# Token scores of six batches: the transposed tokens made by VectorE and a trip through DRAM, eight products of 64 rows in place of 64 products of 32 rows, and a new order of the loop

## The chip, the core and the metric

The kernel runs on one core of a Trainium2 chip. A core has TensorE (PE in the profile: matrix products, with PEld for its weight loads), VectorE (DVE), ScalarE (ACT), GpSimd (POOL) and SyncE (SP, which here only issues transfers). They run at the same time and wait for each other by semaphores. Matrix products write into PSUM, which is cut into banks; everything else lives in SBUF or in DRAM. The metric is the time of one execution in microseconds (us) on the device. Lower is better.

## What is computed

Two stages follow each other. The first is a cross attention between 512 tokens `x` and 32 states in each of 8 batches and 8 heads of 64 features, in both directions:

```python
scores = scale * np.matmul(x, state.transpose(0, 1, 3, 2))     # 512 x 32 per batch and head
a = softmax(scores)                                            # over the 32 states
xread = np.matmul(a, state)
scores2 = scale * np.matmul(state, x.transpose(0, 1, 3, 2))    # the same numbers, transposed
a2 = softmax(scores2)                                          # over the 512 tokens
sread = np.matmul(a2, x)
```

The 512 rows of `xread` and the 32 rows of `sread` of a batch are put one after the other, with the 8 heads side by side as 512 features. The second stage is a gated feed-forward network over these 4352 rows (8 batches of 544): each row is divided by its root mean square and scaled by `rms_g`, multiplied by `w_gate` and by `w_val` (512 by 1536 each), the gate goes through `g * sigmoid(g)`, the two are multiplied, and the product goes through `w_out` (1536 by 512). All of it is float32.

## The kernel before

**Loop.** Batch 0 and the preparation of the weights run first, in an order of their own (`ORDER`). Then a loop over `b` from 1 to 7 does the feed-forward network of batch `b`'s tokens and, beside it, the attention of batch `b + 1`. I call one pass a turn. The 256 state rows of all batches come last (`STATES`).

**Order.** The work of a turn is written as generators, each a stream named by a letter, and the string `PERIOD` says letter by letter whose next step is issued. TensorE, VectorE and ScalarE keep the order that this string gives. GpSimd and the transfer queues of SP get theirs from the planner of the language, by dependencies. The streams are:

- `h`: TensorE's products of the hidden layer (`hidden_seven`, L734). There are six pairs of weight blocks per batch, and each pair has seven products in place of eight, in banks called x, y and z. The steps of a pair are x, z, then s1 (into x), s2 (into z), y, s3 (into x) and the last (into x).
- `t`: ScalarE's copies of the x, z and again x banks (L780, L783, L785) and the gate function (L787). `u`: VectorE's sums for the same pair (L796, L799, L811, L815, L821).
- `p`: the projection by `w_out` (`project_seven`, L896), also with seven products, each in two halves of 12 passes. `c`: ScalarE's copies of finished halves (L933), `k`: VectorE's sums of them (L941, L948), followed by the stores.
- `v` and `w`: TensorE's products that fold the states into the gate and value weights (`own_weights`, L588), which needs weights loaded by SP (`fetch`, L176). `x`: ScalarE's copies of them (L599) and GpSimd's sums (L614 to L617).
- `a`: the token side of the attention of the next batch (`tokens_read`): scores, softmax over states, read of the states (L458), square, mean and root (`rms_on_blocks`, L395 to L406, then L278 on GpSimd and L285), and the scaling of the weights (L471).
- `s`: the state side (`states_read`): softmax over tokens, a transpose by way of DRAM (L512, L515, L519), the read of the tokens (L530), and its transpose (L542).

**Scores of batches 2 to 7.** `scores_of_blocks` works on 32 by 32 blocks. [...] the states are loaded four times, once for each group of 32 partitions (`load_fours`, L114), and transposed as `stB` (L337); the tokens are transposed as `xB` by two instructions (L343). The contraction over 64 features is then split in two halves of 32 rows: 64 products of 32 rows by 32 columns over 128 tokens (L354), into four banks, two of the pool `aps` ("at") and two of the pool `vps` ("pv"). VectorE transposes each bank back into `eS` (L365) and ScalarE copies each into `sS` (L368). For L458 and the scaled weights the states are transposed once more by TensorE (L435). Tokens are loaded so that a partition group holds the tokens that this order needs (L122).

**Scores of batches 0 and 1.** `scores` has the whole transpose: one transpose of the states by TensorE (L296), 16 of the tokens by TensorE with copies by ScalarE (L306, L308), and eight products of 64 rows by 512 tokens (L315) into two banks.

**Buffers.** `aps`, `vps` and `fx` hold two banks each, `fy` and `fz` one. `xT`, which holds `xB` and later the squares, is a single buffer in SBUF. Loaded weights have three.

Of the kernel before, what the change touches and what calls it, by code (L numbers as in the profile page):

```python
# [8 lines left out]
F32 = mybir.dt.float32  # L9
# [8 lines left out]
P = 128  # L18
# [13 lines left out]
    "hhvttvhtxhuhuhxuxthuhtthuhhuthxhuxhuuhtthahuuthtuhuvhxutauhhtxutxhhuuhxhthvuuthh"  # L32
    "axttxuhuuhthuhxhuuuutahhuahutthtuuhuahuuhupaatuauhauupucaaaasaaaaaaapsacksppsasc"
    "aappacaacakpkakaupsaasaacaaspsakksaaaspkkpasawwsspxwxxckpxsxksxc"
# [9 lines left out]
def kernel(  # L44
# [55 lines left out]
    fours = {}  # L100
# [8 lines left out]

    def load_fours(b):  # L110

        fours[b] = one.tile([P, H, D], F32, name="fours")
        for g in range(4):
            nc.sync.dma_start(out=fours[b][Ns * g:Ns * g + Ns],  # L114
                              in_=state[b].rearrange("h n d -> n h d"))
# [37 lines left out]
    w_d = [scratch.tile([P, NI, 2, 2, P], F32, name="w_d%d" % mp) for mp in range(NM // 2)]  # L153
    e_d = [scratch.tile([4, Ns, 4, 8 * Ns], F32, name="e_d%d" % k) for k in range(2)]
# [136 lines left out]
    def scores(b, packed, soft):  # L291

        xb = x_sb[b]
        stT = one.tile([P, 4, Ns], F32, name="stT")
        tp = aps.tile([P, 4, Ns], F32, name="at")
        TE.transpose(out=tp.rearrange("p j n -> p (j n)"),  # L296
                     in_=packed.rearrange("p e d -> p (e d)"), identity=ident)
        yield
        VE.tensor_copy(stT, tp)
        yield "step"  # L300

        xT = one.tile([P, 4, NC, P], F32, name="xT", tag="xT")
        for c in range(NC):
            tp = aps.tile([P, 4, P], F32, name="at")
            for j in range(4):
                TE.transpose(out=tp[:, j, :], in_=xb[:, c, P * j:P * j + P], identity=ident)  # L306
            yield
            SE.copy(xT[:, :, c, :], tp)  # L308
            yield "step"


        sp = [aps.tile([P, S], F32, name="at") for e in range(2)]
        for j in range(4):
            for e in range(2):
                TE.matmul(out=sp[e][Ns * j:Ns * j + Ns, :], lhsT=stT[D * e:D * e + D, j, :],  # L315
                          rhs=xT[D * e:D * e + D, j].rearrange("p c t -> p (c t)"),
                          start=True, stop=True)
        yield


        sS = read[b] = two.tile([P, 2, NC, P], F32, name="sS")
        eS = soft["e"] = one.tile([P, 2, S // Ns, Ns], F32, name="eS", tag="eS")
        for e in range(2):
            VE.transpose(out=eS[:, e].rearrange("p k n -> p (k n)"), in_=sp[e])
            yield
            SE.copy(sS[:, e].rearrange("p c t -> p (c t)"), sp[e])
            yield "step" if e else None

        soft["st"] = stT
        soft["half"] = lambda e: eS[:, e]  # L330
        soft["back"] = lambda e: [(aT_s[b][:, e], eS[:, e].rearrange("p k n -> p (k n)"))]

    def scores_of_blocks(b, packed, soft):

        xb = x_sb[b]
        stB = one.tile([P, H, 2, Ns], F32, name="stB")
        VE.transpose(out=stB.rearrange("p h k n -> p (h k n)"),  # L337
                     in_=fours.pop(b).rearrange("p h d -> p (h d)"))
        yield

        xB = one.tile([P, NC, H, 2, Ns], F32, name="xB", tag="xT")
        for i in range(0, NC, 2):
            VE.transpose(out=xB[:, i:i + 2].rearrange("p c h k t -> p (c h k t)"),  # L343
                         in_=xb[:, i:i + 2].rearrange("p c f -> p (c f)"))
            yield


        sp = [(aps, vps)[g // 2].tile([P, 2, NC, Ns], F32, name=("at", "pv")[g // 2])
              for g in range(4)]
        for e in range(2):  # L350
            for k in range(2):
                for j in range(4):
                    for g in range(4):
                        TE.matmul(out=sp[g][Ns * j:Ns * j + Ns, e].rearrange("n c t -> n (c t)"),  # L354
                                  lhsT=stB[Ns * g:Ns * g + Ns, 2 * j + e, k, :],
                                  rhs=xB[Ns * g:Ns * g + Ns, :, 2 * j + e, k, :],
                                  start=(k == 0), stop=(k == 1), skip_group_check=True)
        yield

        sS = read[b] = two.tile([P, 2, NC, P], F32, name="sS")
        eS = one.tile([P, 4, 2, NC, Ns], F32, name="eS", tag="eS")
        for g in (2, 3, 0, 1):
            VE.transpose(out=eS[:, g].rearrange("p e c n -> p (e c n)"),  # L365
                         in_=sp[g].rearrange("p e c t -> p (e c t)"))
            yield
            SE.copy(sS[:, :, :, Ns * g:Ns * g + Ns], sp[g])  # L368
            yield "step" if g == 1 else None
        soft["half"] = lambda q: eS[:, 2 * q:2 * q + 2].rearrange("p g e c n -> p (g e c) n")  # L370
        soft["back"] = lambda q: [(aT_s[b][:, :, P * g:P * g + P],
                                   eS[:, g].rearrange("p e c n -> p e (c n)"))
                                  for g in (2 * q, 2 * q + 1)]
# [41 lines left out]
    def tokens_read(b):  # L415
        packed, soft = rows.pop(b), {}
        yield from (scores if b < 2 else scores_of_blocks)(b, packed, soft)
        half = soft["half"]
# [6 lines left out]
        for e in range(2):  # L425
            VE.reduce_max(out=m1[:, e], in_=half(e), axis=AXX)
            yield
            VE.tensor_tensor(out=half(e), in0=half(e), in1=along(m1, e), op=ALU.subtract)
            yield
            SE.activation(out=half(e), in_=half(e), func=ACTF.Exp, scale=SCALE)  # L430
            yield "step"
        stT_g[b] = two.tile([P, 4, Ns], F32, name="stT_g")
        if b > 1:
            soft["st"] = aps.tile([P, 4, Ns], F32, name="at")
            TE.transpose(out=soft["st"].rearrange("p j n -> p (j n)"),  # L435
                         in_=packed.rearrange("p e d -> p (e d)"), identity=ident)
            yield
        VE.tensor_tensor(out=stT_g[b], in0=soft["st"], in1=rms_g.unsqueeze(2).to_broadcast([P, 4, Ns]),
# [3 lines left out]
        for e in range(2):  # L442
            VE.reduce_sum(out=z1[:, e], in_=half(e), axis=AXX)
# [4 lines left out]
            VE.tensor_tensor(out=half(e), in0=half(e), in1=along(z1, e), op=ALU.mult)  # L448
            yield
            for to, blocks in soft["back"](e):  # L450
                VE.transpose(out=to, in_=blocks)
# [23 lines left out]
    def states_read(b):  # L475
# [13 lines left out]
        for e in range(2):  # L489
            to = e2[:, :, e].rearrange("p g c t -> p c g t")  # L490
            if b < 2:
                to = exps[:, e]
            SE.activation(out=to, in_=sS[:, e].rearrange("p c (g t) -> p c g t", t=Ns)
                          if b > 1 else sS[:, e], func=ACTF.Exp, scale=SCALE,
# [544 lines left out]
    for b in range(1, B):  # L1039
# [3 lines left out]
        if b + 1 < B:  # L1043
            load_fours(b + 1)
# [58 lines left out]
```

## Time and profile before

| | |
|---|---|
| time, median of 3 | 791.25 us (790.87 to 791.53) |
| profiled execution | 791.0 us, span 789.2 us, granted clock 0.998 |
| batch 0 and preparation, 0 to 141.5 us | TensorE busy 133.3 us |
| one turn, b = 1 to 6 | 85.38 us each, TensorE busy 84.92, VectorE 58.65, ScalarE 31.37, GpSimd 23.6 |
| last turn and state rows, from 653.8 us | 77.6 and 57.8 us |
| VectorE transposes | 128x256: 0.42 to 0.45 us; 128x512: 0.70; 128x1024: 1.24 |
| transfers, issue to landing | 1 MB of weights 5.2 us; 0.5 MB written by `e_d<-eB` 2.9; 128 KB read by `e2T<-e_d` 3.0 |

A page of the profile gives the busy time of each engine, the chain of work that ended last (followed back from the end, at each step to what released it), and groups of equal instructions by line. A row of the chain reads: start in us, length in us, engine, tile, line, number of instructions. In the rows of windows the first column is the stretch, then its length and each engine's busy time with its number of instructions. A product in float32 is two instructions ("passes") in the trace, so 64 products are 128 rows of matmul. "PE f L896" is TensorE writing a tile named `f` at line 896. "ACTq" and "SPq" are the sequencers of ScalarE and SyncE issuing a transfer.

The six turns from b = 1 to 6 have the same length to 0.01 us.

### The profile page before, as it was taken

The numbers are of one execution on the slowest core, as the hardware profiler recorded it, in microseconds if no ns is written. First come the engines' busy times: TensorE is split into PE (matmuls) and PEld (weight loads), VectorE is DVE, ScalarE is ACT, GpSimd is POOL, SyncE is SP. The second block draws the span as 40 slices with busy tenths as digits, with TensorE's granted clock in tenths as the row PEclk, the third lists the DMA queues.
The fourth block names the chain that finished last, engine by engine and source line by source line (L and its number), as shares of the span: only waits on it lengthen the run. The fifth ranks groups of instructions, "written<-read, shape, count | busy, mean of one in ns | idle before, by whom it ended". The sixth has DMA issues, their size and how long they took to land.

```text
span 789.2 us, 13508 instructions
## 1 busy us (share of the span) xinstructions
PE 774.4 (98%) x5394; PEld 593.0 (75%) x5394; DVE 545.2 (69%) x858; ACT 327.6 (42%) x548; POOL 173.8 (22%) x232
## 2 busy tenths in 40 slices
PE   6999999999999999999999999999999999999998
PEld 5643444788777877888778877787788877888996
DVE  4999997689538871888368953887288835781461
ACT  5998864543145322543154314432254315410320
POOL 2100003530164004410443016400441044300000
PEclk9999999999999999999999999999999999999999
DMA  9878864730274025521453038402521143201311
GB/s 287 235 272 302 276 191 167 218 122 1 87 243 168 2 70 180 182 69 43 151 184 121 0 92 255 152 1 68 206 100 55 41 157 126 105 7 41 114 54 27
DMA packets 73599, 102.07 MB, mean 129 GB/s; under 512 B 46913, under 2 KB 57665, under 8 KB 66625
## 3 DMA queue, kind: packets, MB, share of 16 engines
q1 hardware_dynamic: 67040, 94.33, 36.5%
q10 hardware_dynamic: 6496, 6.88, 2.8%
q8 instruction: 43, 0.70, 0.4%
q14 instruction: 20, 0.16, 0.1%
HBM read 82.84 MB, written 18.35 MB: 128 GB/s over the span
## 4 chain that ended last, share of the span: by engine, by line
PE 94%; DVE 2%; ACT 2%; issue 0%; DMA 0%; SPq 0%
PE f L734 38%; PE f L896 35%; PE f L836 5%; PE pv L630 4%; PE at L588 3%; PE pv L588 3%; PE at L530 1%; PE at L458 1%; PE at L354 1%; PE f L987 1%; PE pv L354 1%; PE at L285 0%; DMA rows<-in_state_dram 0%; PE at L306 0%; ACT ex L225 0%
## 5 line engine op out<-in xcount | busy, mean ns | idle before, releaser
L896 PE MATMUL f<-wo,hb 128*128 128x256 f32 x540 | 123.5, 381 | 3.0 <-ACT ot L933 3.0
L734 PE MATMUL f<-aT_s,v 128*128 128x256 f32 x504 | 122.5, 384 | 0.0
L896 PEld LDWEIGHTS f<-wo,hb 128*128 128x128 f32 x540 | 102.1, 190 | 18.9 <-ACT ot L933 5.6
L734 PEld LDWEIGHTS f<-aT_s,v 128*128 128x128 f32 x504 | 93.7, 190 | 24.9 <-issue 12.2
L796 DVE TENSOR_TENSOR g<-g,f 128x512 f32<-128x512 f32 (+1 forms) x96 | 61.9, 652 | 65.2 <-PE f L734 61.8
L734 PE MATMUL f<-aT_t,vs 128*128 128x256 f32 x336 | 87.1, 382 | 0.0
L933 ACT COPY ot<-f 128x256 f32<-128x256 f32 x60 | 21.3, 368 | 157.5 <-PE f L896 157.5
L896 PE MATMUL f<-wt,hs 128*128 128x256 f32 x360 | 82.2, 382 | 0.0
L278 POOL TENSOR_TENSOR ri<-ss,mhalf 128x4 f32<-128x4 f32 x8 | 9.3, 1157 | 330.5 <-DVE ss L406 223.8
L896 PEld LDWEIGHTS f<-wt,hs 128*128 128x128 f32 x360 | 67.3, 190 | 13.9 <-ACT ot L933 4.9
L787 ACT ACTIVATE hb<-g 128x1024 f32<-128x1024 f32 (+1 forms) x48 | 48.2, 1004 | 67.6 <-DVE g L796 67.6
L734 PEld LDWEIGHTS f<-aT_t,vs 128*128 128x128 f32 x336 | 63.3, 190 | 14.8 <-issue 5.9
L614 POOL TENSOR_TENSOR vs<-v 128x256 f32<-128x256 f32 x42 | 30.4, 725 | 137.3 <-ACT v L599 137.2
L799 DVE SCALAR_TENSOR_TENSOR hb<-hb,g 128x1024 f32<-128x1024 f32 x42 | 52.3, 1245 | 5.9 <-ACT hb L787 5.9
L785 ACT COPY g<-f 128x512 f32<-128x512 f32 (+1 forms) x48 | 26.9, 560 | 55.3 <-PE f L734 55.3
L599 ACT COPY v<-pv 128x512 f32<-128x512 f32 x42 | 23.7, 598 | 60.0 <-PE pv L588 60.0
L836 PE MATMUL f<-wo,hb 128*128 128x512 f32 x96 | 44.7, 600 | 0.0
L617 POOL TENSOR_TENSOR vs<-v,vs 128x256 f32<-128x256 f32 x42 | 44.7, 1063 | 0.0
L630 PE MATMUL pv<-aT_s,v 128*128 128x512 f32 x96 | 43.6, 594 | 0.0
L734 PE MATMUL f<-aT_t,v 128*128 128x256 f32 x168 | 43.1, 379 | 0.0
L734 PE MATMUL f<-aT_s,vs 128*128 128x256 f32 x168 | 43.1, 379 | 0.0
L896 PE MATMUL f<-wt,hb 128*128 128x256 f32 x180 | 42.6, 387 | 0.0
(152 smaller groups left out, 1290.9 us busy)
## 6 DMA issues: line engine op xcount, KB each, us to landing
w_m<-w_d SPq DMA_DIRECT2D x48, 1024.0 KB, 5.2
out_dram<-ot SPq DMA_DIRECT2D x56, 128.0 KB, 1.8
raw<-in_moe_w_val_dram SPq DMA_DIRECT2D x6, 1024.0 KB, 5.4
raw<-in_moe_w_out_dram SPq DMA_DIRECT2D x6, 1024.0 KB, 8.0
x_b<-in_x_dram SPq DMA_DIRECT2D x96, 64.0 KB, 2.5
w_d<-w_m SPq DMA_DIRECT2D x6, 1024.0 KB, 4.9
raw<-in_moe_w_gate_dram SPq DMA_DIRECT2D x5, 1024.0 KB, 7.1
e_d<-eB ACTq DMA_DIRECT2D x6, 512.0 KB, 2.9
```

What stands on the lines that cost most here:

```text
L588: TE.matmul(out=pv[e][Ns * j:Ns * j + Ns, :], lhsT=stT_g[b][D * e:D * e + D, j, :], rhs=w[D * e:D * e + D, j].rearrange("p m k f -> p (m k ...
L599: SE.copy(v[:, e].rearrange("p m k f -> p (m k f)"), pv[e])
L614: GE.tensor_tensor(out=vs[:, 0], in0=a21, in1=a22, op=ALU.add)
L617: GE.tensor_tensor(out=vs[:, 2], in0=a12, in1=vs[:, 1], op=ALU.subtract)
L630: TE.matmul(out=to[0], lhsT=lhs(i, k), rhs=r, start=(i == 0), stop=(i == len(rhs) - 1))
L734: TE.matmul(out=ps[:, i, 0:half], lhsT=l[:, i, :], rhs=r, start=(start and i == 0 and k == 0), stop=(k == len(lhs) - 1), skip_group_check= ...
L785: SE.copy(gates(q)[1], q["x"][:, :, 0:half])
L787: SE.activation(out=hb[:, 2 * mp:2 * mp + 2, 0:n].rearrange("p m (c t) -> p m c t", c=2), in_=q["g"][:, :, :, 0:half], func=ACTF.Silu if s ...
L796: VE.tensor_tensor(out=to, in0=to, in1=q[ps][:, :, 0:half], op=ALU.add)
L799: VE.scalar_tensor_tensor(out=h, in0=h, scalar=1.0, op0=ALU.add, op1=ALU.mult, in1=q["g"].rearrange("p m c t -> p m (c t)"))
L836: TE.matmul(out=banks[r], lhsT=hb[:, m, P * r:P * r + P], rhs=wo[:, m, :], start=(m == 0), stop=(m == NM - 1))
L896: TE.matmul(out=banks[name][:, r, :], lhsT=lhs(k)[:, P * r:P * r + P], rhs=rhs(k), start=(start and r == 0 and k == 0), stop=(k == HM - 1) ...
```

## The change

For batches 2 to 7, `scores_of_blocks` and its lines L354, L337 and L343 go, and so does `load_fours` with its four loads per batch. `scores` now serves all batches. The states are transposed by TensorE at the start (L289 of the new file) and copied by VectorE (L292); the scaled weights use that copy, so the later transpose (L435 before) goes.

For the tokens, VectorE transposes the 32 by 32 blocks of one 128x512 slice at a time (four instructions, writing runs of 32 numbers), ScalarE's queue writes the result to a buffer in DRAM, and four more transfers on the same queue read it back so that every partition holds one feature of a pair of heads: a full transpose. The eight products of 64 rows by 512 tokens then go into two "at" banks.

```diff
+    x_d = [scratch.tile([4, 4, Ns, 4 * P], F32, name="x_d%d" % k) for k in range(2)]
...
+            xB = one.tile([P, 4, 4, NC, Ns], F32, name="xB", tag="xT")
+            for c in range(NC):
+                VE.transpose(out=xB[:, :, :, c, :].rearrange("p q j t -> p j q t"),
+                             in_=xb[:, c].rearrange("p (j q t) -> p j q t", j=4, t=Ns))
+                yield
+            nc.scalar.dma_start(out=x_d[b % 2].rearrange("q g f r -> (g f) q r"),
+                                in_=xB.rearrange("p q j c t -> p q (j c t)"))
+            yield
+            xT = one.tile([P, 4, 4, P], F32, name="xG", tag="xT")
+            for q in range(4):
+                nc.scalar.dma_start(
+                    out=xT[Ns * q:Ns * q + Ns].rearrange("f g j r -> f g (j r)"),
+                    in_=x_d[b % 2][q].rearrange("g f r -> f g r"))
+                yield
+            xT = xT.rearrange("p g j r -> p j g r")
...
-        for e in range(2):
-            for k in range(2):
-                for j in range(4):
-                    for g in range(4):
-                        TE.matmul(out=sp[g][Ns * j:Ns * j + Ns, e].rearrange("n c t -> n (c t)"),
-                                  lhsT=stB[Ns * g:Ns * g + Ns, 2 * j + e, k, :],
-                                  rhs=xB[Ns * g:Ns * g + Ns, :, 2 * j + e, k, :],
-                                  start=(k == 0), stop=(k == 1), skip_group_check=True)
...
-                for to, blocks in soft["back"](e):
-                    VE.transpose(out=to, in_=blocks)
+                VE.transpose(out=aT_s[b][:, e], in_=eS[:, e].rearrange("p k n -> p (k n)"))
...
-        if b + 1 < B:
-            load_fours(b + 1)
```

`xB`, `xG` and later the squares share the single buffer `xT`. The copies out of the score banks, the transposes back and the softmax work on halves of 128x512 in place of quarters of 128x256.

`PERIOD` is new. The `a` stream has 46 steps in place of 43. What moves in it:

- The transposes of the tokens and the write to DRAM stand between the first and second pair of the hidden layer; in the old order the two transposes stood from the third to the fifth. The four reads stand among the copies of the fifth and sixth pairs.
- The scores stand after the hidden layer's last step, between the two halves of the first projection; before, they stood between the fifth and sixth pairs.
- Of the weight products of a turn (`v`), the second and third are issued one after the other, before the second pair's y step; before, the first and second were.
- The copy of the first projection's first half (`c`) stands before its second half is computed. Both copies of the third use of the x bank stand before the next product into it; before, the second copy stood between that product's halves.
- The read of the tokens (L530 before) stands ahead of the next batch's two weight products (`w`), which follow each other; before, one was ahead of it and one between the halves of the last projection.

In the built program each transfer has one of eight semaphores, dealt in turn, and waits for the transfer that had it before. In five of the six turns SP's load of the sixth pair's weights gets the one that the write of `x_d` had.

## The prediction

> **What bounds the kernel now.** I read the page's busy shares, then the chain that ended last, then the windows of single turns (one pass of the batch loop), then the chain inside one turn.
>
> ```profile
> PE 774.4 (98%) x5394; PEld 593.0 (75%) x5394; DVE 545.2 (69%) x858; ACT 327.6 (42%) x548; POOL 173.8 (22%) x232
> ...
> PE 94%; DVE 2%; ACT 2%; issue 0%; DMA 0%; SPq 0%
> ...
> 312.29:397.67 85.38, 84.92 (x650) 68.06 (x649) 58.65 (x95) 31.37 (x58) 23.60 (x29) 1.00 0.36 116
> ...
> 64.02 1.02 PE at L315 x16
> ...
> 336.31 6.24 PE f L734 x28
> 342.55 0.23 PE at L354 x2
> ...
> 344.38 6.24 PE f L734 x28
> ...
> 370.78 5.39 PE f L896 x24
> 376.17 0.02 issue
> 376.19 0.38 ACT ot L933
> 376.57 0.04 issue
> 376.61 2.86 PE f L896 x12
> 379.47 0.13 PE at L401 x2
> ```
>
> TensorE carries 94% of the chain, and a turn repeats every 85.38 us, of which it is busy 84.92. DVE has 26.7 us free per turn, ACT 54. So only two things move the time: work that leaves TensorE, and places where TensorE waits. The chain inside a turn shows one of each. The scores of blocks (L354) hold it from 342.55 to 344.38, 1.83 us. At 376.17 it stands for ACT's copy of the second half of a projection bank.
>
> **What the Trainium skill says.** "TensorE: Matmul & The Clock Gate", Part 3: matmuls in different tiles of the array run concurrently, and each adds about 4 ns of issue. The trace agrees in direction: L354's 128 passes of mean 278 ns fit in 1.83 us, but they start 13 to 33 ns apart, so many small tiles cost more than few long ones. "PSUM — Partial Sum Buffer", PSUM bank collisions: engines are to be kept apart by bank, not address. The trace agrees: ACT's copy at 376.19 reads the half finished at 373.4, and started only when the other half's 12 matmuls ended at 376.17. "SBUF — State Buffer", Who interferes with whom: a VectorE instruction with one SBUF input doesn't contend with GpSimd. The trace agrees: L337's transpose at 322.63 took 0.70 beside busy POOL, its mean; L811 with two inputs took 1.10 beside POOL and 0.69 without.
>
> **The change part by part.** Times are us from the turn's first product (308.69 in the trace's turn).
>
> *Scores.* Removed: 64 products of 32 rows by 128 columns, 1.83 us on the path. Added: eight of 64 rows by 512 columns. That form is in the trace: L315, batches 0 and 1, 16 passes in 1.02 us. All of it lies on the path: 1.02 − 1.83 = −0.81 per turn, six turns. The step back to full-array products costs about 0.20 in both (344.38: 28 passes of 0.2156 are 6.04, and took 6.24).
>
> *State transpose* L435 becomes L296: 0.11 both times, moved to the turn's start; its copy adds 0.29 to DVE, hidden as below.
>
> *The half banks.* In the new order both copies (L933) of the x bank's third use (two in a row: 0.62 in the trace at 363.55) stand before the next product into that bank, and the read products of L458 (1.05) stand between. 0.02 + 0.65 = 0.67 of copying lies beside 1.05 of reads, so the wait goes. What it cost: from 376.17 to 379.47 are 3.30 us for 12 passes, which elsewhere take 2.59: −0.71 per turn, six times. In the last turn two state passes (0.22) fill part of the wait: about −0.5.
>
> *Next batch's two weight products.* Before, one follows the reads and one stands alone between projections (390.15, with 2.79 instead of 2.59 behind it). Now both follow L530 directly: one change of array shape fewer, −0.20 per turn. The second needs two "at" banks: along_rows' is free after L471 (1.22) and L530's after L538 (0.48). From along_rows' end these are done at 1.75; the product starts at 2.05. Margin 0.3, so nothing.
>
> *A new wait on a half.* The copy of the first bank's first half (L933) now stands ahead of that bank's second half, so TensorE, and with it everything behind, waits for it. The first half ends at 42.7, ACT is free of its last gate function at 41.5, so the copy runs 42.75 to 43.1; the second half stands at 44.8, behind one L734 step and the scores. Margin 1.7, nothing.
>
> *Last turn.* The state norm's steps ride on the same letters and move to the turn's start. L555 costs 1.68 on TensorE at either place; its input square (1.06 on ACT) is done at 6.0 and L555 stands at 7.3. Nothing.
>
> *DVE.* Removed per turn: stB 0.70, xB 2×1.24, eS 4×0.44, back 4×0.42 = 6.62. Added: copy 0.29, four xB of 128x512 at 0.70 (L337's form), eS 2×0.69 (L324), back 2×0.70 (L451's large form) = 5.87. So −0.75, all off the path, if the xB transposes, which write runs of 32 numbers, cost what contiguous ones cost. The trace shows no such write: bounds 0.6 (nothing excludes a gain of some 0.1) and 1.4 (double). I take 0.70, since L451, writing two runs, equals contiguous forms.
>
> *The DMA by way of DRAM.* ACT's queue gets one write (1 MB; issue 0.35 as L515) and four reads (256 KB; 0.44 each as L519): 2.1 us of ACT, which has 54 free. What stands behind them matters. The transposes run at 7.2–8.6 and, behind L799 (1.3), 9.9–11.3. The write waits for the last on ACT, ahead of the copy of the second pair's x bank, which so runs 11.7–12.3; the product that needs it starts at 13.9, because two weight products (2.04) now stand ahead. Margin 1.6. The DVE steps pushed back give: third x bank needs L811 done by 14.75, is done 13.1; the second pair's last product needs L796 by 16.5, done 15.5. Margin 1.0, the thinnest here.
>
> Landing: w_d<-w_m, also 1 MB, 4.9 us; twice e_d's 2.9 gives 5.8. I take 5: 16.5. In the built order SP's next weight load (the sixth pair's, 1 MB) waits in five of the six turns for the write's semaphore, and behind it on SP stand the next batch's two weight loads and later stores. It then lands at 16.5 + 5.2 = 21.7, or 24 at the 7.6 that was the longest seen for w_d in that stretch; its product stands at 26.8. Margin 2.8 to 5. The reads are issued from 30.7 to 36.9 between copies; with e2T's 3.0 for half the size, x_b's 6.8 for the same size, the last lands at 40 to 43.7; the scores stand at 43.55. I take 40, since x_b's 6.8 fell into the crowded start. No more waits are met on ACT's queue (write landed at 16.5, reads from 30.7).
>
> *SP.* fours' four loads per turn go: 1.9 us of SP's queue at 251.47, nothing on the path. sS copies, exponentials in other shapes: ACT, same sizes, nothing; they stand beside projections.
>
> *Order after the scores.* eS, maxima and the rest stretch from 44.6 to 60.9; L458 stands at 62.9. L948's first half waits for a projection to 49.95 (DVE idle 1.7), which the margin of 2.0 already contains. The pow and along_rows: 0.13 + 0.75 + 1.02 beside 2.59. Nothing.
>
> Sum: 6×(0.81 + 0.71 + 0.20) + 0.5 = 10.8. Span 789.2 − 10.8 = 778.4; that execution was timed 791.0, 1.8 more than its span, and the median of three is 791.25. So 791.25 − 10.8 = **780.4**, turns of 83.66.
>
> **The rivals.** Beyond 0.2% (1.6 us) counts as a difference.
>
> A, *thin margins are partly used up* (0.3, 1.0 and others near it): each lost wait of 0.3 to 1 us per turn returns 2 to 6. Gives 783 to 787, say 785. For: PEld already shows waits of up to 0.9 at copies. Against: the old order runs on similar margins with one wait.
>
> B, *strided transposes cost double*: four times 0.7 on DVE by 11.3 moves the write to 14.2. ACT's copy ends at 15.2 instead of 13.9 (−1.3), the L796 step adds 0.3: 1.6 per turn, 9.6 in all. Gives 790, about no change. Against: L451.
>
> C, *the write through DRAM is slow, and SP with it.* 2 KB pieces to DRAM, then the weight load held behind it: place is the sixth pair's weight product. Decides from landing 10.3 us after issue (26.8 − 5.2 − 11.3); every us beyond costs 5 in all. Slower than before from 12.5. At 15 us: 780.4 + 23.5 = 804. For: nothing else of this write's pattern is in the trace, and x_b with 256 B pieces ran 6.8. Against: 1 MB in 4.9.
>
> D, *the change doesn't do what it says*, i.e. the half banks still wait (copies late behind ACT's exponentials): 780.4 + 4.8 = 785, within A's figure. Against: ACT is idle there before the copies (5.6 at 369.77).
>
> **How the numbers follow.** Forecast 0.58, A with D 0.20, B 0.07, C 0.12, and 0.03 for below 778.5. The forecast's own range is 779 to 782.5. To leave two in ten out, A must be in: 778.5 to 787.5 holds 0.58 + 0.20 and a little of B. Faster: 0.58 + 0.20 + 0.03 + 0.03 of B = 0.84. Same: 0.04 of B. Slower: C's 0.12.
>
> **What would show it.** Right: the scores at 1.0 in the chain, no ACT copy in it between L458 and the L896 behind it, turns of 83.7. The four xB transposes at 0.7 each. The write landing near 5, with SP's weight load issued behind it. Wrong: TensorE idle before the second pair's s3 product (B), before the sixth pair's weight product with a DMA named as releaser (C), before the scores (reads late), or before the second of the next batch's weight products (A).

## The result: 779.5 us, turns of 83.48 us, and where 11.7 us went

| | before | after |
|---|---|---|
| time, median of 4 runs | 791.24 us (790.87 to 791.53) | 779.5 us (778.67 to 779.63) |
| ratio, with its 95% interval | 1 | 0.985 (0.9833 to 0.9867) |
| span of the profiled execution | 789.2 us | 777.7 us |
| start to the state-read transpose (`sr`) of batch 1 | 135.75 us | 136.26 us |
| first of the six turns | 87.45 us | 85.55 us |
| each of the other five | 85.38 us | 83.48 us |
| from the transpose of batch 7 to the end of the chain | 135.91 us | 135.40 us |

The small transpose (`sr`, L542 before, L502 after) closes a turn's attention and is one clear row per turn in the chain, so I measure turns from it to the next. The first of the six is 2.07 us longer in both kernels, because work of the first stage (1.72 us of it at L836 before) still lies behind that transpose. The parts add up: six turns by 1.90 us are 11.4, the last turn gives 0.51, and the first stage takes 0.51 back. The 0.1 us that is missing to the 11.5 of the span lies behind the chain, in the last stores.

The busy shares and the engines of the chain that ended last, from the page of the kernel after:

```profile
PE 765.8 (98%) x4722; PEld 586.2 (75%) x4722; DVE 536.7 (69%) x846; ACT 325.6 (42%) x536; POOL 161.6 (21%) x232
...
PE 92%; DVE 5%; DMA 1%; SPq 1%; issue 0%; ACT 0%; DVEq 0%
```

TensorE lost 672 instructions (5394 to 4722), six times the 112 passes that the scores lost (128 to 16), but only 8.6 us of busy time. The shares of ACT (2% to 0%) and DVE (2% to 5%) differ mostly in the first stage, where the chain is followed back through VectorE's preparation of the weights in one trace and through ScalarE's in the other. The window of one turn of the kernel after (columns as in the window shown of before):

```profile
307.12:390.60 83.48, 83.48 (x545) 66.98 (x551) 57.29 (x93) 31.04 (x56) 21.63 (x29) 1.00 0.42 139
```

TensorE has not one idle stretch in the turn: 83.48 of 83.48. Before it was 84.92 of 85.38. So of the 1.90 us about 1.44 left as TensorE's own time and 0.46 as visible idle time. (The copies' wait cost more than the 0.46 shown as idle: in the chain shown of before, TensorE stands 0.44 us, and the 12 passes after it take 2.86 in place of 2.59.) The chain inside the same turn of the kernel after:

```profile
348.87 1.02 PE at L328 x16
349.89 18.33 PE f L856 x84
368.21 0.59 PE at L421 x4
...
369.26 7.97 PE f L856 x36
377.23 0.13 PE at L370 x2
377.36 2.69 PE f L856 x12
380.04 0.44 PE at L278 x4
380.48 1.03 PE at L490 x64
381.51 1.02 PE pv L548 x16
382.53 0.86 PE at L548 x16
```

Read it against the chain of before. The scores are L328 with 1.02 us, where L354 took 1.83. Between the reads (L421) and the small product (L370) stand 36 passes in one piece, with no "issue" and no ACT row between them: 36 by 0.2156 are 7.76, and the 0.2 left over is the step back from the small shape. The next batch's weight products (L548) follow the state read (L490) without anything between. The second of them takes 0.86, not 1.02. Where the two copies went is seen on ScalarE's timeline of the kernel after:

```profile
368.25 0.37 ACT L893 COPY ot<-f 128x256 f32<-128x256 f32 x1 [8.27 <-PE f L856]
368.52 0.38 ACT L893 COPY ot<-f 128x256 f32<-128x256 f32 x1
```

They run from 368.25 to 368.90, beside the reads, which start at 368.21 and end at 369.26.

The account of a turn: −0.81 (scores), −0.71 (copies), −0.20 (one change of shape fewer), −0.16 (the second weight product) make −1.88 of the measured −1.90.

### The profile page after: what moved, and what is told of

It reads as the page before. It is cut to its first block, busy times and chain, and to the rows that moved or that the text cites. A ratio compares the mean times of both kernels' runs of the same rounds, so it can differ in the third digit from the quotient of the medians.

```text
span 777.7 us, 12111 instructions
## 1 busy us (share of the span) xinstructions
PE 765.8 (98%) x4722; PEld 586.2 (75%) x4722; DVE 536.7 (69%) x846; ACT 325.6 (42%) x536; POOL 161.6 (21%) x232
## 4 chain that ended last, share of the span: by engine, by line
PE 92%; DVE 5%; DMA 1%; SPq 1%; issue 0%; ACT 0%; DVEq 0%
PE f L694 38%; PE f L856 35%; PE f L796 5%; PE pv L590 4%; PE at L548 3%; PE pv L548 3%; PE at L328 1%; DVE ex L249 1%; PE at L490 1%; PE at L421 1%; DVE raw L245 1%; DMA raw<-in_moe_w_gate_dram 1%; DVE w_m L254 1%; DVE top L242 1%; DMA rows<-in_state_dram 0%
## 5 line engine op out<-in xcount | busy, mean ns | idle before, releaser
L694 PE MATMUL f<-aT_s,v 128*128 128x256 f32 x504 | 119.7, 382 | 0.0
L856 PE MATMUL f<-wt,hs 128*128 128x256 f32 x360 | 80.4, 379 | 0.0
L796 PE MATMUL f<-wo,hb 128*128 128x512 f32 x96 | 44.7, 600 | 0.0
L856 PE MATMUL f<-wo,hs 128*128 128x256 f32 x180 | 41.5, 382 | 0.0
L856 PE MATMUL f<-wt,hb 128*128 128x256 f32 x180 | 40.8, 383 | 0.0
```

Source lines behind the costliest of these rows:

```text
L694: TE.matmul(out=ps[:, i, 0:half], lhsT=l[:, i, :], rhs=r, start=(start and i == 0 and k == 0), stop=(k == len(lhs) - 1), skip_group_check= ...
L796: TE.matmul(out=banks[r], lhsT=hb[:, m, P * r:P * r + P], rhs=wo[:, m, :], start=(m == 0), stop=(m == NM - 1))
L856: TE.matmul(out=banks[name][:, r, :], lhsT=lhs(k)[:, P * r:P * r + P], rhs=rhs(k), start=(start and r == 0 and k == 0), stop=(k == HM - 1) ...
```

## The experiments

Two of the twelve kernels start from the kernel before, ten from the kernel after. The start of the program up to the first turn differs by up to 1.4 us from kernel to kernel (135.3 to 136.7 us), also where nothing there was edited, so I give turns beside times. A ratio is to the kernel before as it ran beside that experiment (medians of 790.77 to 791.55 us), and "ahead of" and "behind" mean the order of issue. Single letters of `PERIOD` are the streams named above.

### The copies and the wait behind them

**One copy put back.** Of the changed kernel only one letter `c` of `PERIOD` moves, from ahead of the product to between its halves. (The two copies are those called `u2` in the source. They are the third pair of copies, and hold what the second product into the x bank left; "the third use of the x bank" in the texts above means this pair.)

```diff
-    "aaaapkkcpccaakaaascuskaappkaaaaap..."
+    "aaaapkkcpccaakaaasuskaapcpkaaaaap..."
```

> The changed kernel with one step put back: ScalarE's second copy of the half banks of the third use of x (u2) comes again between the two halves of the next product into that bank, the reads of the state stay where they are, so nothing lies between the first copy and the first half but the reads, and nothing between the halves but the second copy. Theory (the wait for the copy is what the change took off, and the bank is guarded as a whole): each of the six turns 0.7 us longer, 84.2 instead of 83.48 us from v2 to v2, and some 0.5 us in the last turn, 784.3 us in all, with TensorE idle on ScalarE at the second product's half. Rival D (the dependence is by halves, or the wait was hidden): the turns stay at 83.48 us and the time at 779.5 us. A half effect, only the copy's own 0.37 us, would give 782.

Measured: 784.31 us, ratio to before 0.9911 (0.9896 to 0.9926); turns of 84.21 us, +0.73. The chain of that run:

```profile
370.68 2.80 PE f L856 x12
373.48 0.02 issue
373.50 0.38 ACT ot L893
373.88 0.04 issue
373.93 5.45 PE f L856 x24
```

ACT stands on the path again, as in the kernel before. TensorE stands 0.44 us, and the rest of the 0.73 is again in the passes behind the wait. In this program the copy waits for the whole bank: the half that it reads was done before the reads of the state, and it starts 0.02 us after the product into the other half has ended. Where it stands decides 0.73 us, so rival D, that the wait is still there in the changed kernel, is out.

**The copies alone, in the old kernel.** The same placing in the kernel before, both copies and then the reads behind both halves of the product:

```diff
-    "aappacaacakpkakaupsaasaacaaspsakksaaaspkk..."
+    "aappacaakpccakakaupsaasaaaaspsakksaaaspkk..."
```

> The kernel before with one part of the change alone: both copies of the half banks of the third use of x and then the reads of the state stand ahead of the next product into that bank; the scores, the transposes and the places of the weight products stay as before. Theory: 0.7 us a turn and 0.5 us in the last, so turns of 84.67 instead of 85.38 us and 786.4 us in all. Rival (the gain came from the dealt order or the scores and this wait was worth little): turns of 85.2 to 85.4 us, 790 to 791 us. Rival (the copies now hold back the reads, which stand behind the rest of the product before): turns longer than 85.4 us.

Measured: 790.23 us, ratio 0.9987 (0.998 to 0.9994); turns of 85.34 us, −0.04. I had expected −0.7, so the theory in this form fell. ACT did leave the path, and TensorE's timeline of that run names what came in its place:

```profile
378.20 0.37 PE L401 MATMUL at<-part,groups 128*128 128x16 f32 x2
378.97 5.45 PE L896 MATMUL f<-wo,hs 128*128 128x256 f32 x24 [0.41 <-DVE hs L948]
```

The projection's product behind the next one reads `hs`, which VectorE subtracts (L948) after the three sums of squares, a transpose and a reduction. The reads moved back by one half product, the squares with them, and L948 with the squares. The chain of the same run shows the column of work that TensorE now waits for:

```profile
376.62 0.72 DVE sq L395
...
377.37 0.69 DVE part L398
378.05 0.88 DVE hs L948
378.93 0.04 issue
378.97 2.21 PE f L896 x9
```

**The copies, and VectorE's subtractions ahead of the squares.** The kernel before with the same move of the copies, and two letters `k` moved ahead of the squares, where the new order also has VectorE run them:

```diff
-    "aappacaacakpkakaupsaasaacaaspsakksaaaspkk..."
+    "aappacaakpccakakaupsaaskkaaaaspsasaaaspkk..."
```

> The kernel before with the two copies ahead of the reads, as in the run of that part alone, and in addition VectorE's two subtractions for the next product (the second use of `less`) ahead of the squares' sums, as the changed kernel has them. The run of the copies alone gained only 0.04 us a turn, and its trace names these subtractions as what TensorE waits for (0.4 us in each of six turns, and 0.6 by the distance of the products). Theory (the copies' wait had a second wait right behind it, which the reads' later place makes worse): turns of 84.7 instead of 85.34 us, 786.4 us in all. Rival (another step of VectorE's chain from the squares ends last, the partial sums ahead of the small product): 85.2 to 85.4 us, 790 us. Rival (the copies are worth nothing in the old kernel): 85.38 us.

Measured: 786.96 us, ratio 0.9946 (0.993 to 0.9963); turns of 84.77 us, −0.61. The chain of this run has one column of TensorE from the reads to the weight product:

```profile
372.13 5.38 PE f L896 x24
377.51 0.24 PE at L401 x2
377.75 5.28 PE f L896 x24
```

That settles it for the old order: two moves had to be made together, and the copies alone paid almost nothing. The 0.1 us that is missing to 0.71 stands in the second row: L401, which needs the reduction of the squares' sums, takes 0.24 in place of 0.13.

### The weight products side by side

**Apart again.** One letter `w` of the changed kernel moves behind the first half of the last projection product:

```diff
-    "...aaksapkakasswwwxxpxkxxpccssx"
+    "...aaksapkakasswwxxpwxkxxpccssx"
```

> The changed kernel with one step put back: the first half of the projection's last product stands again between the two weight products of the next batch. The prediction priced the two changes of shape saved at 0.20 us a turn: 83.68 us a turn, 780.7 us in all. With the trace of the changed kernel the second of two adjacent weight products also takes 0.86 instead of 1.02 us: together 0.36 us a turn, 83.84 us, 781.7 us in all. If the place does not matter: 83.48 and 779.5 us.

Measured: 781.84 us, ratio 0.9879 (0.9864 to 0.9893); turns of 83.83 us, +0.36. So adjacency is worth 0.36, not the 0.20 of the prediction: the step back to the full array is saved (0.20), and the step into the small shape too (0.16, the 1.02 of a first product against the 0.86 of a second).

**One more pair.** If 0.36 us per group is right, a turn with two groups in place of three is shorter. Of the four products of `v`, the changed kernel issues one alone, two together, one alone. Here all four stand in pairs, with the copies that belong to them moved along:

```diff
-    "hhvthttxhauhhxhuauaahhtutaahtahvxvtuhuxxhuuhthtxuthuhtuhhuhuhhutuhutthuxuhxtxuhh"
-    "vhuuthhxthxtahuhathuuuxuuauthuthtahhuthuuuhuhpuuuhtuuucauapaaasaspkacpaspsspaaaa"
+    "hhthtthauhhhuauaahvvhtuthtxxxtxxaaahuhuhuuhthtxuthuhtuhhuhuhhutuhvvutthuxuhxtxuh"
+    "hhuuthhxthxtahuhathuuuxuuauthuthtahhuthuuuhuhpuuuhtuuucauapaaasaspkacpaspsspaaaa"
```

> The changed kernel in another order: the weight products of the third and fourth pair stand together ahead of the last product of the first pair, those of the fifth and sixth together ahead of the last product of the third, so that there are two groups in place of three. If a change of shape costs 0.20 us and the second of two adjacent weight products is 0.16 us shorter, a turn loses 0.36 us: 83.12 us and 777.3 us in all. Against it: the copies of the fourth pair's weights come later on ScalarE, and the products of the second pair may wait for GpSimd's sums; a wait of over 0.4 us a turn takes it all back, 779.5 us or more.

Measured: 777.61 us, ratio to before 0.9829 (0.9812 to 0.9845); turns of 83.26 us, −0.22 in place of −0.36. It is the fastest of all these kernels. Its interval overlaps that of the kernel after, so the difference is carried by the turns: from the transpose of batch 1 to the end it takes 636.81 us, the kernel after 638.33. The chain of this run:

```profile
388.36 3.60 PE f L694 x16
...
392.07 3.46 PE f L694 x16
395.52 1.02 PE pv L548 x16
396.54 0.86 PE at L548 x16
...
410.55 1.02 PE pv L548 x16
411.56 0.86 PE at L548 x16
```

Both pairs show 1.02 and 0.86. But the first row takes 3.60 for 16 passes, and the second 3.46 for as many: 0.14 us are lost where a turn begins. The weight product that stood there until now gave ScalarE time to copy the first bank before the third product writes into it. That the copy is the cause is argued from its place (on ScalarE's timeline it ends at 389.84, just when that product is due, at about 389.9), and not shown: the trace names no wait that short.

The Trainium skill says in "TensorEngine Tiling (Array Packing)", Key Properties, that a change of tiling mode (of the shape of the pieces into which the array is divided), not of the tile alone, drains TensorE. It gives no price. The runs agree that a change costs time, and give the price for this shape: 0.36 us for the way in and out, in two parts of 0.16 and 0.20.

### What made the old scores slow

The change made 64 products of 32 rows into eight of 64 rows, so two things fell together. Three kernels take them apart, all in the place of the changed kernel's scores.

**32 products of 64 rows:**

```diff
+            for g in range(4):
+                for j in range(4):
+                    for e in range(2):
+                        TE.matmul(out=sp[e][Ns * j:Ns * j + Ns, P * g:P * g + P],
+                                  lhsT=stT[D * e:D * e + D, j, :],
+                                  rhs=xT[D * e:D * e + D, j, g], ...)
```

> The changed kernel with the scores of the six turns in 32 products of 64 rows by 128 columns instead of eight by 512 columns; operands and results are the same. It separates the two things that fell together when 64 products became eight: the number of products and the height of the stack of rows. If the number of products costs (0.01 to 0.03 us for each product more than the columns need): 64 passes instead of 16 take about 1.37 us, 0.35 us a turn, turns of 83.83 us, 781.6 us in all. If only the height of 32 rows costs, the scores stay at 1.02 us and the time at 779.5 us. If the products by 128 columns are as slow as those of 32 rows were: 1.83 us, turns of 84.29, 784.4 us.

Measured: 779.73 us, ratio 0.9852 (0.9835 to 0.9868); scores 1.09 us, turns of 83.54 us, +0.06.

**16 products of 32 rows,** with all 512 columns. The halves go to different banks and are not added, so half of the sum is left out:

```diff
+            sq = [vps.tile([P, S], F32, name="pv") for e in range(2)]
+            for j in range(4):
+                for e in range(2):
+                    for k in range(2):
+                        r = slice(D * e + Ns * k, D * e + Ns * k + Ns)
+                        TE.matmul(out=(sq if k else sp)[e][Ns * j:Ns * j + Ns, :],
+                                  lhsT=stT[r, j, :], rhs=xT[r, j], start=True, stop=True)
```

> The changed kernel with the scores of the six turns in 16 products of 32 rows by 512 columns: each half of the contraction apart, the second halves into two other banks. The two halves are not added and the second is read by nobody, so this leaves out half of the sum; the columns that pass are as many as in the kernel before (64 products of 32 rows by 128 columns). It tells whether the 1.83 us of before came from the height of 32 rows or from the number of products. If the height: 1.7 to 1.83 us for the scores. If the number: about 1.02 us, turns of 83.48 us.

Measured: 779.07 us (one run); scores 1.07 us (348.25 to 349.32 in the chain), turns of 83.53 us, +0.05. At 512 columns, height alone costs 0.05 us.

**64 products of 64 rows by 64 columns:**

```diff
+            for g in range(8):
+                for j in range(4):
+                    for e in range(2):
+                        TE.matmul(out=sp[e][Ns * j:Ns * j + Ns, D * g:D * g + D],
+                                  lhsT=stT[D * e:D * e + D, j, :],
+                                  rhs=xT[D * e:D * e + D, j, g // 2, D * (g % 2):D * (g % 2) + D], ...)
```

> The changed kernel with the scores of the six turns in 64 products of 64 rows by 64 columns; operands and results are the same as with eight. The run with 32 products took 1.09 us for 64 passes, 0.07 more than eight products: 17 ns from pass to pass, which can be the columns' own time or just the floor of a start. 128 passes in 1.83 us were 14.3 ns each before. If a start has such a floor: 1.8 to 2.2 us here, turns of 84.3 to 84.7 us. If only the columns count: 1.02 to 1.2 us, turns of 83.5 to 83.7 us.

Measured: 781.99 us (one run), turns of 83.87 us, +0.39; the chain of this run gives the scores 1.41 us:

```profile
349.77 1.41 PE at L336 x91
```

(The chain counts only 91 of the 128 passes, though the trace has all of them; the length is that up to the next piece, at 351.18.) The answer lies between the two that I had written down. 112 more passes cost 0.39 us, 3.5 ns each. That is close to the 4 ns of issue per tile that the page cited in the prediction states, though here it is passes that were added, in the same eight tiles of the array. It does not explain the old form: as many passes, but 32 rows high and 128 columns long, took 1.83. Number explains 0.39 of the 0.81, height by itself 0.05. The remaining 0.37 belongs to the two together, or to something else in which the old form differed: it added two halves in one bank, and alternated between four banks. No run here separates these.

### VectorE's transposes at double cost

Rival B priced the strided transposes at double. They came out at 0.686 us each (24 of them, 15.6 us), as the prediction assumed. So the price of B could only be tested by doing them twice:

```diff
+                for again in range(2):
+                    VE.transpose(out=xB[:, :, :, c, :].rearrange("p q j t -> p j q t"),
+                                 in_=xb[:, c].rearrange("p (j q t) -> p j q t", j=4, t=Ns))
```

> The changed kernel with VectorE's four block transposes of x done twice each (same result, the work repeated): 4 times 0.69 = 2.7 us more VectorE work a turn, which is what rival B supposed if a strided transpose costs double. The prediction's arithmetic for B: 1.6 us a turn, turns of 85.1 us, 789 us in all. Read again from the trace of the changed kernel, where VectorE waits for little ahead of the transposes: 0.7 to 1.0 us a turn, turns of 84.2 to 84.5 us, 784 to 785.5 us. If VectorE has room there: 83.48 and 779.5 us.

Measured: 787.37 us, ratio 0.9953 (0.9938 to 0.9968); turns of 84.83 us, +1.35. The chain of this run shows the place:

```profile
405.85 0.72 DVE xB L311
...
406.59 0.38 ACTq L314
...
407.01 0.59 ACT g L746
...
407.65 1.56 PE f L695 x6
```

It is the one that the prediction described: the last transpose, the issue of the write on ScalarE's queue, the bank copy that stands behind that issue, and the product that needs the copy. VectorE's 2.74 us more (4 by 0.686) became 1.35, so the room was 1.4 us. The prediction had said 1.6. Of the 1.6 per turn that it gave for B, 1.3 were for this place, and 0.3 for a second one (the L796 step) that did not appear. TensorE's own timeline shows only 1.08 us of idle time here; the other 0.27 are in the passes behind the wait (1.56 for the six in the last row, which elsewhere take 1.29), as they were behind the wait for the copy (2.86 for twelve in place of 2.59).

### A slower write to DRAM

Rival C: SyncE's weight load stands behind the write's semaphore, nothing is lost until the write lands 10.3 us after issue, and each us beyond costs one in five turns. One transfer that writes the same data several times makes the landing longer. Three runs have three, four and six copies, of which the first is read back. The run with four:

```diff
-    x_d = [scratch.tile([4, 4, Ns, 4 * P], F32, name="x_d%d" % k) for k in range(2)]
+    x_d = [scratch.tile([4, Ns, 4, 16 * P], F32, name="x_d%d" % k) for k in range(2)]
...
+            nc.scalar.dma_start(out=x_d[b % 2].rearrange("g f d s -> (g f) d s"),
+                                in_=xB.rearrange("p q j c t -> p (q j c t)").unsqueeze(1)
+                                .to_broadcast([P, 4, 16 * P]))
```

> The changed kernel with the write of the transposed x to DRAM made longer: one transfer writes three copies, of which the first is read back (the other two are never read). 3 MB instead of 1 MB: an estimate from the 4.3 us of 1 MB is a landing of 9 to 10 us after issue. Theory C of the prediction: SyncE's weight load stands behind this write's semaphore in five of six turns, and nothing is lost until the write lands 10.3 us after its issue: 779.5 us. From the trace of the changed kernel the point lies nearer, at some 8.5 us, because the load itself takes 5.7 us: 0.5 to 1.5 us in five turns, 782 to 787 us. If SyncE is not held by it: 779.5 us.

> The changed kernel with the write of the transposed x as one transfer of four copies, 4 MB, of which the first is read back. From 4.3 us for one, 9.2 for three and 17.4 for six the landing is estimated at 12 us after issue. The prediction's point of 10.3 us: 1.7 us in each of five turns, 788 us. The point of 11.0 us, read from the run with six copies (17.5 us of landing, TensorE waiting 6.5): 1.0 us in five turns, 784.5 us. If the 2 us a turn that the run with six copies lost beyond its wait, with the products behind it at twice their length, come with every wait and not only with a long one: 10 us more, 794 us or over.

> As the run with three copies, with six: 6 MB, landing estimated at 16 to 18 us after issue. Theory C: five turns longer by what the landing is beyond 10.3 us, 6 to 8 us each, 810 to 818 us in all; with the point at 8.5 us 7.5 to 9.5 us each, 817 to 827 us. In the five turns TensorE waits ahead of the weight product of the sixth pair. If SyncE is not held by the write, only the reads of x behind it can be late: issued 24 us after the write, so nothing: 779.5 us.

| copies | median landing after issue | time, median of 4 | ratio to before | turns of the profiled execution, beyond 83.48 us (first: 85.55) |
|---|---|---|---|---|
| 1 (kernel after) | 4.3 us | 779.5 us | 0.985 (0.9833 to 0.9867) | none |
| 3 | 9.2 us | 778.64 us | 0.9844 (0.9829 to 0.9859) | none |
| 4 | 11.7 us | 785.71 us | 0.9933 (0.9914 to 0.9951) | 1.5, 0.9, 4.6, 0.7, 0.8, none |
| 6 | 17.4 us | 830.57 us | 1.05 (1.0484 to 1.0516) | 8.3, 9.0, 8.4, 8.1, 8.7, 8.8 |

The profiled execution with four copies was the slowest of its four: 788.04 us, where the others took 784.40 to 785.73.

The 0.9 us by which three copies look faster is all in the start: from the transpose of batch 1 to the end both take 638.33 us. With six copies the chain runs as rival C has it:

```profile
333.94 17.54 DMA x_d<-xB
...
351.50 0.02 SPq L169
...
351.56 4.78 DMA w_m<-w_d
...
356.38 1.96 PE at L549 x16
```

The write lands, SyncE's sequencer goes on in the same instant, and the weight load that it then issues is what TensorE's sixth-pair product waits for. The Trainium skill has this in "DMA: Bandwidth & Descriptors", Anatomy of one DMA — SWDGE (gpsimd) path: the DMA engines do not wait on semaphores, the sequencer that issues the transfer does. TensorE stood 6.5 us (32.4 us in five turns), so the point from which it costs is 17.5 − 6.5 = 11.0 us. With four copies it is 11.7 − 0.8 = 10.9. The prediction's 10.3 had taken 5.2 for the load; it took 4.7 to 4.9 in four of the five turns. In the first it took 5.1 and 5.2, and there the point does lie at 10.3 (16.7 − 6.4 with six copies, 11.7 − 1.5 with four). My reading from the trace of after, 8.5 us, was wrong: it used the load's median of 5.7 us, and other loads of that line are slower than this one. The last turn of the run with four copies is free of the loss, as the prediction's five of six says, though its write took 18.8 us. With six copies the last turn is hit in another way: that write took 26.3 us, and the first read back waited for it on ScalarE's queue with a bank copy behind it (`ACT g L746`, after the DMA in the chain).

But a turn lost 8.1 to 9.0 us with six copies, while TensorE stood only 6.5. The product behind the wait also took 1.96 in place of 1.02. The windows of this run, ahead of the wait and behind it (the granted clock is the third number from the end, 1.00 in the first row and 0.50 in the second):

```profile
345.00:349.80 4.80, 4.80 (x23) 3.94 (x21) 3.69 (x5) 2.55 (x6) 2.50 (x4) 1.00 1.00 420
356.40:358.30 1.90, 1.90 (x17) 0.24 (x17) 0.00 (x0) 0.00 (x0) 0.00 (x0) 0.50 1.01 427
358.30:360.30 2.00, 2.00 (x11) 1.64 (x6) 0.00 (x0) 0.58 (x1) 0.00 (x0) 0.54 1.02 430
360.30:364.00 3.70, 3.70 (x19) 3.26 (x18) 1.89 (x3) 2.15 (x4) 2.37 (x3) 1.00 0.99 360
```

The mean of 0.54 in the third row puts the end of the slow stretch at about 360.1, so TensorE worked some 3.7 us at half its clock, which costs another 1.9. The clock had fallen while TensorE still stood: it is 1.00 from 349.9 to 353.3 and 0.50 from 353.4 on. The run with four copies has shorter waits. Its TensorE timeline has them ahead of the sixth pair's product, here in three turns:

```profile
165.63 1.09 PE L549 MATMUL at<-w_m,stT_g 64*32 64x512 f32 x16 [1.47 <-DMA w_m<-w_d]
...
249.99 1.09 PE L549 MATMUL at<-w_m,stT_g 64*32 64x512 f32 x16 [0.81 <-DMA w_m<-w_d]
...
336.34 1.09 PE L549 MATMUL at<-w_m,stT_g 64*32 64x512 f32 x16 [2.81 <-DMA w_m<-w_d]
337.36 1.76 PE L695 MATMUL f<-aT_s,v 128*128 128x256 f32 x4
338.92 1.91 PE L695 MATMUL f<-aT_t,vs 128*128 128x256 f32 x4
```

After 0.81 and 1.47 us of waiting the turns lost 0.9 and 1.5, about what the wait lasted. After 2.81 us four passes show 1.76 and 1.91 us where they usually show 1.03, and the turn lost 4.6. The windows of that turn have the granted clock at 0.50 (again the third number from the end), from 1.4 us after the wait's end and for 3.4 us:

```profile
336.34:337.72 1.38, 1.38 (x18) 0.52 (x19) 0.13 (x1) 0.15 (x1) 0.00 (x0) 1.00 1.02 433
337.72:341.13 3.41, 3.41 (x10) 2.70 (x9) 0.00 (x0) 1.78 (x4) 0.72 (x1) 0.50 0.99 408
```

This was seen in one turn of one execution. Of the other three only the mean granted clock is known, 0.999 to 1.0.

The Trainium skill says in "TensorE: Matmul & The Clock Gate", Part 1, that the array drops to half its clock after at least one idle window of about 3.4 us, and needs about as long to come back. The halving agrees in both runs. So does the time to come back: 3.7 us of work with six copies, and a slow stretch of 3.4 us with four. With six copies the clock fell some 3.4 us after TensorE had stopped (at 349.86), which fits the idle window. The wait of 2.81 us does not: it was shorter than the page's window, and the clock fell all the same. Why is not shown.

## Why the prediction was right, and where it was not

**Right in the number, 780.4 against 779.5 us.** The sum of 10.8 us stands against 11.5 in the span. That is closer than the terms were. Over the six turns and the last one the change took 11.9 us off, 1.1 more than the sum; the 0.5 us by which the start of this execution was longer, which nobody had forecast, hid nearly half of that. This part of the agreement is luck.

- *Scores*: −0.81 predicted, 1.02 us in the chain, as read from L315. The size is right. The reason that the prediction hinted at, many small tiles, explains only half of it (0.39), and the rest is open. The prediction's 13 to 33 ns between starts of L354 are those of products, which are two passes each: 128 passes in 1.83 us are 14 ns each.
- *The half banks*: −0.71 per turn, measured +0.73 when one copy is put back, and −0.5 in the last turn, measured −0.51. The size is right, but the step as written was incomplete. It said that the copies lie beside the reads, "so the wait goes". In the old kernel that was done, and another wait took the place of the first: VectorE's subtraction L948 stood right behind. There the time came only when L948 also went ahead of the squares' sums. The new `PERIOD` has this order too; that the changed kernel would lose the gain without it is argued and was not run. The prediction, which asked when the first use of L948 is ready, never asked that of the second.
- *The weight products*: the term that was mis-sized. Predicted −0.20 per turn, measured 0.36. Only the step out of the small shape was counted. The 0.86 was there to be read in the chain of before, where two such products followed each other, and the mean over the line hid it (rows below). Six times 0.16 is 1.0 us, more than the whole error of the prediction.

```profile
395.80 1.02 PE pv L588 x16
396.81 0.86 PE at L588 x16
```

- *VectorE's transposes*: 0.70 assumed, 0.686 measured. Margin of the copy behind them: 1.6 predicted, 1.4 measured.
- *The trip through DRAM*: landing of the write 5 predicted, 4.3 measured; SyncE's load behind it, as predicted, in five of six turns; reads back 3 assumed, 5.0 measured (2.9 to 6.3), within the bounds named and without effect. In the turn shown the last read was issued at 341.14 and the scores began at 348.87, so even the slowest read (6.3 us) would have left 1.4 us.
- *The second weight product's margin of 0.3 and the 1.0 at the second pair*: TensorE has no idle stretch in the turn shown, so there was no wait at either, and A did not come.
- *What was not foreseen*: the first stage took 0.5 us longer. Over all kernels that start lay anywhere between 135.3 and 136.7 us, so I do not put it down to the change.

**The rivals.** A and D did not occur; D's price, 4.8 us, was measured as 4.8 by putting the copy back. B did not occur; its price would have been 7.9 us, not 9.6. C did not occur; its point (10.3 us) was nearly right (11), but its price of 5 us per us holds only for short waits. At waits of 2.8 us and over, a turn lost 1.5 to 2.4 us more than TensorE stood. At a landing of 15 us TensorE would wait some 4 us in five turns; with 2 us more each, that is an estimate of 30 us from these two runs, in place of the 23.5 given.

## What to carry to other kernels

When a wait is taken away, look for the one that stands right behind it: ask of every instruction between the moved work and the next product when it would be ready if the first wait were gone. A change of array shape has a price on the way in and on the way out, so put small products of one shape side by side, and read single rows of the chain rather than means over a line to find what they cost. A wait of TensorE can cost more than the trace shows as idle: up to 1.5 us it cost what it lasted and up to 0.27 us more in the passes behind it, while one of 2.8 us and those of 5.7 to 7.5 us were followed by a stretch at half the clock.

## What the runs showed of the hardware that I had not expected

- TensorE behind a wait: full clock after 0.8 and 1.5 us of standing still, half the clock after 2.8 us (seen once) and after 5.7 to 7.5 us (in five turns of one execution). The slow stretch lasted 3.4 us after the wait of 2.8; with a wait of 6.5 it began within the wait and took some 3.7 us of the work behind it.
- Number of products in the small shape: 112 passes more, each of an eighth of the columns, cost 0.39 us. A height of 32 rows in place of 64 cost 0.05, as long as the products were 512 columns long.
- Length of a write of SBUF to DRAM by one transfer: median 4.3, 9.2, 11.7 and 17.4 us for 1, 3, 4 and 6 MB, so 2.5 to 2.9 us for each MB from three up. (The 1 MB goes out in pieces of 2 KB, the others in pieces of 8 KB.) In the last turn the same write took 13.6 (3 MB), 18.8 (4 MB) and 26.3 us (6 MB).
